# First head pair's bias loads on GpSimd's queue, and the fourth unit's exponentials ahead of the last value parts

## The chip, the cores and the metric

The program runs on one core of one Trainium2 chip. The metric is device microseconds (us) of one execution, as the median of several. TensorE (PE) multiplies matrices, VectorE (DVE), ScalarE (ACT) and GpSimd (POOL) work elementwise, SyncE (SP) here only issues DMAs. POOL and ACT can issue DMAs too. PEld is PE's loading of weights.

## The reference, cut to what matters

Attention with a bias that a small network computes from positions, then a feed-forward part with a convolution and a gate:

```python
scores = scale * np.matmul(q, k.transpose(0, 1, 3, 2))        # (4, 8, 576, 576)
x = (psi_rel / psi_i)[..., None]                              # (576, 576, 1)
h = np.maximum(x @ w1 + b1, 0.0)                              # 32 hidden units
scores = scores + (h @ w2).transpose(2, 0, 1)[None, :, :, :]  # a bias for each of 8 heads
attn = np.exp(scores - np.max(scores, axis=-1, keepdims=True))
attn = attn / (np.sum(attn, axis=-1, keepdims=True) + 1e-09)
x = np.matmul(attn, v)                                        # then heads are joined: (4, 576, 512)
h = np.maximum(x @ w_in, 0.0)
out = (h * sigmoid(conv3(h))) @ w_out
```

The bias does not depend on the batch. It is computed once, for all heads, and used four times.

## The kernel before, in words

**Bias stage.** A loop of 36 blocks (index i, `NBLK`) computes the bias, 16 rows of positions a block. For a block DVE (L250) and ACT (L246) compute four tiles `y` of hidden units, PE (L267) multiplies them by `w2` into PSUM, and for each pair of blocks ACT (L293) writes the result to a staging tile `st` (five of them in turn, one called `tl`), which SP stores to `bias_d` in HBM (L306, 607 KB a pair of blocks). The blocks are software-pipelined: in step i the program first emits the hidden tiles of block i+1, then the matmuls of block i, then `bias_out` of block i-1.

**Bias tiles.** Attention reads the bias back from HBM, as tiles `bt` of 128 rows for a head pair p and row group t = 0 to 4, by `load_bias(p, t)`: two DMAs, one for each head (L183 for t = 0, which has 64 rows for each head, 144 KB each; L181 for the others, 288 KB each). Row group 0 needs blocks 0 to 3, row group 1 blocks 4 to 11, and so on, so each load waits until the stores of its blocks have landed. For the first head pair the loads of t = 0 to 3 stand in the loop at i = 6, 14, 22 and 30 and are issued from SP; for the others POOL issues them. The load of (0, 4) comes after the loop, cut into rows 0 to 95 and 96 to 127.

**Units.** A unit (n, t) is a pair of heads of one batch (n) and a row group (t): PE's scores (L363), DVE's addition of the bias with the row maxima (`reduce`, L374, needs `bt`; it writes `sp` and `nm`), ACT's exponentials (`expo`, L388, one for each head), a small ACT copy that marks the tile as ready for PE (`turned_sp`, L342), PE's transposes (L422 into a PSUM tile shared with the scores of another unit, L434 into tiles `tp`), ACT's and DVE's copies of them to `ptx` and `pty` (L90, L93), and parts of the value product (L471). Four units of n = 0 are worked inside the bias loop, from steps 13, 21, 29 and 34: (0,0), (0,1), (0,2) and (0,3). Of (0,3), the fourth, the loop does only the scores and the two `reduce`.

**After the loop.** The program emits the scores and `reduce` of (1,0), then the value parts still in the deque `fill` (PE, L471, into a PSUM tile named `tp`; the last part ends with ACT's copy of it to `x`, L90 called from L480), then the exponentials of (0,3), then the main loop over `flat` = (0,3), (1,0), (1,1), (0,4), (1,2), ... In its turn u, that loop emits the scores and `reduce` of the unit two ahead, the transposes of unit u and the exponentials of the unit one ahead. Each engine works its instructions in the order in which they are emitted; nothing reorders them.

Of the kernel before, what the change touches and what calls it, by code (L numbers as in the profile page):

```python
# [19 lines left out]
def attention_ffn_kernel(  # L20
# [11 lines left out]
    nc = tc.nc  # L32
# [23 lines left out]
    def halves(ap):  # L56
        return ap.rearrange("p (a b) -> p a b", a=2)
# [79 lines left out]
    with tc.manual_schedule():  # L137
# [9 lines left out]
        def load(n):  # L147
            p, b = seq[n]
            qks[n] = t = q_p.tile([P, KO + S], F32, name="qk")
            keys = qk[b, p, :, KO:].rearrange("d (h a s) -> d a h s", h=2, a=2)  # L150
            for a in range(2):
                rows = slice(D * a, D * a + D)
                nc.sync.dma_start(t[rows, 0:KO], qk[b, p, :, 0:KO])
                nc.sync.dma_start(halves(t[rows, KO:]), keys[:, a])
# [10 lines left out]
        def load_v(n):  # L165
            p, b = seq[n]
            vts[n] = vt = v_t[n % 2]
            by5 = [x.rearrange("p (g s) d -> p g (s d)", s=5)[:, :, 0:4 * D] for x in (vt, v[b, p, :, 0:10])]
            nc.sync.dma_start(*by5)
            nc.sync.dma_start(vt[0:TL, 4], v[b, p, 0:TL, 4])  # L170
            nc.sync.dma_start(vt[TL:P, 9], v[b, p, TL:P, 4])

        def load_bias(p, t, cuts=()):
            queue = nc.gpsimd if p else nc.sync
            bt = bias_p.tile([P, 2, S], F32, name="bt") if t else bias0_p.tile([P, 1, S], F32, name="bt0")
            for a, e in zip((0,) + cuts, cuts + (P,)):
                for h in range(2):
                    c = (2 * p + h) * BW
                    if t:
                        i0 = TL + (t - 1) * P  # L180
                        queue.dma_start(bt[a:e, h], bias_rows[i0 + a:i0 + e, c:c + S])  # L181
                    else:
                        queue.dma_start(bt[TL * h:TL * h + TL, 0, :], bias_rows[0:TL, c:c + S])  # L183
            biast[p, t] = bt
# [52 lines left out]
        def bias_hidden(blk):  # L237
            full = max(reach(blk)[0], reach(blk)[1] + 1)
            ys = []
            for j in range(4):  # L240
                ig = 4 * blk + j
                n = max(S - 4 * ig, 4 * ig + 4) if 4 <= blk < 32 else full
                row = ybuf[blk % 4][:, j] if j < 3 else y3[:, blk % 4]
                y = row[:, 0:n]
                if j >= relu_from(blk):
                    nc.scalar.activation(  # L246
                        y, dist[:, 0:n], AF.Relu, bias=pars[:, 1:2], scale=inv[:, ig:ig + 1]
                    )
                else:
                    nc.vector.tensor_scalar(  # L250
                        y, dist[:, 0:n], inv[:, ig:ig + 1], nb1, op0=ALU.mult, op1=ALU.max
                    )
                ys.append(row[:, 0:full])
            return ys
# [3 lines left out]
        def bias_mm(blk, ys):  # L258
            n = ys[0].shape[1]
            if n > 512 or blk % 2 == 0:  # L260
                bias_ps[blk] = psS.tile([P, 2, 512], F32, name="s")
            else:
                bias_ps[blk] = bias_ps[blk - 1]
            ps = bias_ps[blk]
            for a in range(0, n, 512):
                for j in range(4):
                    nc.tensor.matmul(  # L267
                        ps[32 * j:32 * j + 32, a // 512 if n > 512 else blk % 2, 0:min(n - a, 512)],
                        w2b,
                        ys[j][:, a:min(n, a + 512)],  # L270
                        start=True,
                        stop=True,
                    )
# [55 lines left out]
        def new_sp(n, t):  # L329
            tag = f"sp{len(nms) % SPB}"  # L330
            tile = sp_p.tile([P, 2 * S + 2], F32, name="sp", tag=tag)
            if t:
                spt[n, t] = (tile[:, 0:2 * S].rearrange("p (h j) -> p h j", h=2), tag)
            else:
                if n == 0:
                    nc.vector.memset(tile[:, 0:TL], 0.0)
                    nc.vector.memset(tile[:, TL + S:P + S], 0.0)
                spt[n, t] = (tile[:, TL:TL + S].rearrange("p (h j) -> p h j", h=1), tag)

        def turned_sp(n, t):  # L340
            tile = sp_p.tile([P, 2 * S + 2], F32R, name="sr", tag=spt[n, t][1])
            nc.scalar.activation(tile[:, 2 * S:], pars[:, 0:2], AF.Copy)  # L342
            spt[n, t] = (tile, None)


        def scores(n, t, h):
            p, b = seq[n]
            qt = qks[n]
            if h == 0:
                if n not in sms:  # L350
                    sms[n] = sm_p.tile([P, 9], F32, name="sm")
                nms[n, t] = sm_p.tile([P, 2], F32, name="nm")
                new_sp(n, t)
            ps = psum["s"].tile([P, 2, 512], F32, name="s")


            ops = [(h, h * QW + P * t, slice(0, P))] if t else [
                (hh, hh * (QW + TL), slice(TL * hh, TL * hh + TL)) for hh in range(2)
            ]
            for hh, qo, po in ops:  # L360
                for a in range(2):
                    rows = slice(D * a, D * a + D)
                    nc.tensor.matmul(  # L363
                        ps[po, a, 0:HS],
                        qt[rows, qo:qo + po.stop - po.start],
                        qt[rows, KO + hh * HS:KO + hh * HS + HS],
                        start=True,
                        stop=True,
                    )
            return ps  # L370

        def reduce(ps, n, t, h):
            bt = biast[seq[n][0], t]
            nc.vector.tensor_tensor_reduce(  # L374
                out=halves(spt[n, t][0][:, h]),
                in0=ps[:, :, 0:HS],
                in1=halves(bt[:, h]),
                op0=ALU.add,
                op1=ALU.min,
                scale=-scale,  # L380
                scalar=3.0e38,
                accum_out=nms[n, t][:, h:h + 1],
            )

        def expo(n, t, h):
            sp, nm = spt[n, t][0], nms[n, t]
            col = 4 * h + t - 1 if t else 8
            exps[n, t, h] = nc.scalar.activation(  # L388
                sp[:, h], sp[:, h], AF.Exp, bias=nm[:, h:h + 1], scale=-1.0,
                accum_out=sms[n][:, col:col + 1],  # L390
            )
# [188 lines left out]
        flat = [(n, t) for n in range(1, NSEQ) for t in units]  # L580
# [4 lines left out]
        def heads(t):  # L585
            return (0, 1) if t else (0,)
# [26 lines left out]
        for i in range(NBLK):  # L613
            nxt = bias_hidden(i + 1) if i + 1 < NBLK else None
            bias_mm(i, hidden)
            if last:
                bias_out(*last)
            last = (i,)
            hidden = nxt
            if i % 8 == 6 % 8 and i >= 6:  # L620
                load_bias(0, (i - 6) // 8)
            if i == 2:
                load(0)
            if i == 4:
                load_v(0)
            if i == 16:
                load(1)
            if i == 20:
                load_v(1)
            if i in starts:  # L630
                unit = unit_steps(*first[starts.index(i)])
            if unit:
                next(unit, None)
            for _ in range(max(0, i - starts[-1] + 1)):
                fill.popleft()()
        bias_out(*last)
        load_bias(0, 4, (96,))
        reduce(scores(*flat[1], 0), *flat[1], 0)
        while fill:
            fill.popleft()()  # L640
        early.close()
        psT = pool(ctx, "psT", 3, space=PSUM)
        psO = pool(ctx, "psO", 1, space=PSUM)
        psum.update(s=psS, tp=psT, o=psO)
        for h in heads(flat[0][1]):
            expo(*flat[0], h)
        turned_sp(*flat[0])
        pv_share = (2, 2, 1, 3, 2)
        hs_ff = {}
        raw_w = {}  # L650
# [4 lines left out]
        for u, (n, t) in enumerate(flat):  # L655
            p, b = seq[n]
# [49 lines left out]
            if u + 2 < NU:  # L706
                n2, t2 = flat[u + 2]
                p2, b2 = seq[n2]
                if b2 == B - 1 and p2 + 1 < NP:
                    load_bias(p2 + 1, t2)  # L710
# [228 lines left out]
```

## Time and profile before

| | |
|---|---|
| median of 3 runs | 493.66 us (493.31 to 494.21) |
| profiled execution, its own time | 493.83 us |
| its span, first to last instruction | 492.1 us |
| granted TensorE clock, mean | 1.000 of full speed |
| PE / PEld / DVE / ACT / POOL busy | 478.5 / 353.1 / 376.9 / 311.4 / 154.0 us |
| DMA: SP's and POOL's queues | 47.02 MB and 12.77 MB, 33.2% and 8.8% of 16 DMA engines' span |

The busy times are sums over the whole span. The ends of matmuls are modelled, so that a busy PE is not one at its peak. Outside the span lie 1.7 us of the profiled execution.

### The profile page before, as it was taken

What the parts mean: (1) busy time and instruction counts of PE and PEld (TensorE: products, weight loads), DVE (VectorE), ACT (ScalarE), POOL (GpSimd) and SP (SyncE); (2) the same over time, 40 slices, a digit from 0 to 9 for tenths busy, and PEclk for the clock granted to TensorE, in tenths of its full rate; (3) what the DMA queues carried; (4) which work ended last, traced back from release to release, by engine and by line L of the source; (5) the groups of instructions that cost most, each with busy time, mean ns of one, the idle gap of its engine ahead of it and who ended that gap; (6) DMA issues with size and microseconds to landing.
All of it is one profiled execution on the core that took longest, in us unless ns stands there. A gap on an engine that the chain in (4) does not pass through costs nothing.

```text
span 492.1 us, 11067 instructions
## 1 busy us (share of the span) xinstructions
PE 478.5 (97%) x4202; PEld 353.1 (72%) x4202; DVE 376.9 (77%) x871; ACT 311.4 (63%) x751; POOL 154.0 (31%) x215
## 2 busy tenths in 40 slices
PE   6989999999999999999999999999999999999996
PEld 4333356666666666666666689889988999899986
DVE  6989967788898889988898729944896279838930
ACT  6989877888888889888888736712542144224510
POOL 1000001245455735565547725160081005400000
PEclk9999999999999999999999999999999999999999
DMA  1999667388667895589751300002000300020011
GB/s 38 280 332 318 253 194 172 93 277 214 158 180 201 225 254 157 161 218 290 191 130 50 111 25 26 2 0 87 0 1 0 108 1 1 1 85 1 1 44 64
DMA packets 32584, 60.82 MB, mean 124 GB/s; under 512 B 7196, under 2 KB 15796, under 8 KB 32532
## 3 DMA queue, kind: packets, MB, share of 16 engines
q1 hardware_dynamic: 27380, 47.02, 33.2%
q0 software_dynamic: 4768, 12.77, 8.8%
q8 instruction: 33, 0.54, 0.5%
q10 hardware_dynamic: 384, 0.35, 0.2%
q14 instruction: 19, 0.16, 0.1%
HBM read 44.12 MB, written 15.98 MB: 122 GB/s over the span
## 4 chain that ended last, share of the span: by engine, by line
PE 88%; ACT 5%; DVE 3%; DMA 3%; issue 1%; SPq 0%; DVEq 0%
PE s L536 21%; PE o L471 17%; PE s L363 16%; PE tp L786 16%; PE tp L434 9%; PE o L786 4%; PE s L267 2%; DVE y L250 2%; DMA bias_d<-st 1%; ACT st L293 1%; ACT y L246 1%; ACT sp L388 1%; PE s L422 1%; DVE sp L374 1%; DMA pars<-in_par_dram 1%; DMA bt<-bias_d 1%
## 5 line engine op out<-in xcount | busy, mean ns | idle before, releaser
L374 DVE CUSTOM_DVE_ANT_0 sp<-s,bt 128x576 f32<-128x576 f32 x144 | 104.1, 754 | 32.3 <-PE s L363 13.1
L388 ACT ACTIVATE sp<-sp,nm 128x576 f32<-128x576 f32 x144 | 109.9, 767 | 0.8 <-DVE nm L374 0.8
L536 PEld LDWEIGHTS s<-xs,wi 128*128 128x128 f32 x768 | 102.8, 189 | 1.2 <-issue 0.5
L536 PE MATMUL s<-xs,wi 128*128 128x288 f32 x768 | 103.6, 296 | 0.0
L363 PE MATMUL s<-qk 64*128 64x288 f32 (+1 forms) x640 | 92.6, 431 | 0.5 <-DVE pty L93 0.2
L363 PEld LDWEIGHTS s<-qk 64*128 64x128 f32 (+1 forms) x640 | 46.9, 175 | 42.1 <-DVE nm L374 12.1
L786 PE MATMUL tp<-wo,g 128*128 128x512 f32 x288 | 70.7, 390 | 0.0
L434 PE MATMUL tp<-identr,sr 64*128 64x64 f32 x1184 | 64.3, 247 | 0.0
L786 PEld LDWEIGHTS tp<-wo,g 128*128 128x128 f32 x288 | 53.7, 188 | 11.8 <-DVE g L781 0.9
L434 PEld LDWEIGHTS tp<-identr,sr 64*128 64x128 f32 x1184 | 55.5, 136 | 5.6 <-issue 0.6
L761 DVE SCALAR_TENSOR_TENSOR cv<-h,cw,cv 128x575 f32<-128x575 f32 x64 | 55.2, 863 | 2.5 <-ACT cv L756 0.6
L548 ACT ACTIVATE h<-s 128x576 f32<-128x576 f32 x32 | 20.8, 651 | 55.2 <-PE s L536 55.2
L267 PE MATMUL s<-y,pars 128*32 128x512 f32 (+8 forms) x352 | 46.8, 513 | 4.0 <-DVE y L250 3.4
L250 DVE TENSOR_SCALAR y<-tl,inv,nb 128x576 f32<-128x576 f32 (+33 forms) x112 | 47.6, 506 | 0.1
L471 PE MATMUL o<-ptx,vt 128*64 128x320 f32 x300 | 47.0, 442 | 0.0
L471 PE MATMUL o<-pty,vt 128*64 128x256 f32 x320 | 44.2, 393 | 0.0
L133 POOL TENSOR_SCALAR xs<-x 128x576 fp32r<-128x576 f32 x16 | 15.2, 950 | 81.4 <-PE s L536 66.5
L267 PEld LDWEIGHTS s<-y,pars 128*32 128x32 f32 x352 | 17.3, 115 | 30.6 <-DVE y L250 15.3
L767 ACT ACTIVATE cv<-cv 128x576 f32<-128x576 f32 x32 | 21.8, 680 | 23.6 <-DVE cv L761 23.6
L498 POOL DMA_DIRECT2D r_d<-rt x16 | 10.0, 625 | 82.9 <-DVE rt L93 82.9
L768 DVE SCALAR_TENSOR_TENSOR cv<-cv,h 128x576 f32<-128x576 f32 x32 | 29.6, 924 | 5.7 <-ACT cv L767 5.7
L93 DVE COPY ptx<-tp 128x256 f32<-128x256 f32 (+1 forms) x64 | 32.0, 499 | 1.4 <-PE tp L434 1.2
(83 smaller groups left out, 635.8 us busy)
## 6 DMA issues: line engine op xcount, KB each, us to landing
qk<-in_qk_dram SPq DMA_DIRECT2D x32, 320.0 KB, 5.1
bias_d<-st SPq DMA_DIRECT2D x13, 607.0 KB, 5.0
bt<-bias_d POOLq DMA_DIRECT2D x24, 288.0 KB, 5.5
qk<-in_qk_dram SPq DMA_DIRECT2D x32, 144.0 KB, 5.4
rb<-r_d POOLq DMA_DIRECT2D x32, 144.0 KB, 3.1
vt<-in_v_dram SPq DMA_DIRECT2D x16, 256.0 KB, 5.9
raw_w<-in_moe_w_in_dram SPq DMA_DIRECT2D x16, 256.0 KB, 5.0
out_dram<-o SPq DMA_DIRECT2D x16, 256.0 KB, 2.0
```

The lines of the kernel that those rows point to most:

```text
L93: nc.vector.tensor_copy(o, i)
L250: nc.vector.tensor_scalar(y, dist[:, 0:n], inv[:, ig:ig + 1], nb1, op0=ALU.mult, op1=ALU.max)
L267: nc.tensor.matmul(ps[32 * j:32 * j + 32, a // 512 if n > 512 else blk % 2, 0:min(n - a, 512)], w2b, ys[j][:, a:min(n, a + 512)], start=Tr ...
L363: nc.tensor.matmul(ps[po, a, 0:HS], qt[rows, qo:qo + po.stop - po.start], qt[rows, KO + hh * HS:KO + hh * HS + HS], start=True, stop=True,)
L374: nc.vector.tensor_tensor_reduce(out=halves(spt[n, t][0][:, h]), in0=ps[:, :, 0:HS], in1=halves(bt[:, h]), op0=ALU.add, op1=ALU.min, scale ...
L388: exps[n, t, h] = nc.scalar.activation(sp[:, h], sp[:, h], AF.Exp, bias=nm[:, h:h + 1], scale=-1.0, accum_out=sms[n][:, col:col + 1],)
L434: tr = nc.tensor.transpose(ps[a][:, TL * s:TL * s + TL].bitcast(F32R), spf[ra, j:j + P], identr[ra, ra])
L471: nc.tensor.matmul(po[D * h:D * h + D, 0:width], vt[:, slot, :], pt[:, blk, :], start=(c == 0), stop=(c == 4),)
L536: nc.tensor.matmul(ps[:, a, 0:HS], wi[c][:, pw, cs], xss[b, c][:, px, a * HS:(a + 1) * HS], start=(i == 0), stop=(i == 3 * KC - 1),)
L761: nc.vector.scalar_tensor_tensor(out=cv[:, o:o + S - 1], in0=h[:, i:i + S - 1], scalar=cw[:, f, kk:kk + 1], in1=cv[:, o:o + S - 1], op0=AL ...
L768: nc.vector.scalar_tensor_tensor(out=cv, in0=cv, scalar=1.0, in1=h, op0=ALU.add, op1=ALU.mult)
L786: nc.tensor.matmul(ps, lhs(f, gi), wo[f][:, wj, cs], start=(f == 0 and i == 0), stop=(f == FC - 1 and i == 2),)
```

## The change

Two edits. The queue of a bias load is now chosen by whether it is cut, so the four loads of the first head pair inside the loop go from SP's queue to POOL's, and they are emitted at i = 4, 12, 20, 28, two steps earlier. The cut load (0, 4) stays on SP. And the two exponentials of (0,3) with their `turned_sp` are emitted ahead of the value parts, no longer behind them.

```diff
         def load_bias(p, t, cuts=()):
-            queue = nc.gpsimd if p else nc.sync
+            queue = nc.sync if cuts else nc.gpsimd
...
-            if i % 8 == 6 % 8 and i >= 6:
-                load_bias(0, (i - 6) // 8)
+            if i % 8 == 4:
+                load_bias(0, i // 8)
...
         load_bias(0, 4, (96,))
         reduce(scores(*flat[1], 0), *flat[1], 0)
+        for h in heads(flat[0][1]):
+            expo(*flat[0], h)
+        turned_sp(*flat[0])
         while fill:
             fill.popleft()()
         early.close()
         psT = pool(ctx, "psT", 3, space=PSUM)
         psO = pool(ctx, "psO", 1, space=PSUM)
         psum.update(s=psS, tp=psT, o=psO)
-        for h in heads(flat[0][1]):
-            expo(*flat[0], h)
-        turned_sp(*flat[0])
```

SP's instructions in the first half of the bias loop, before (-) and now (+); `vt` is V, `st` and `tl` are staging tiles, L306 the stores, L183 and L181 the bias loads:

```order
 L171 DMA vt_106<-in_v_dram 64x64
 L306 DMA bias_d<-st_125 128x2x607
-L183 DMA bt_266<-bias_d 64x576 x2
 L306 DMA bias_d<-st_132 128x2x607 x2
 L306 DMA bias_d<-tl 128x2x607
 L306 DMA bias_d<-st_124 128x2x607
-L181 DMA bt<-bias_d 128x576 x2
 L306 DMA bias_d<-st_125 128x2x607
```

The stores keep their order, and the loads that stood between them are gone from SP.

POOL's instructions of the change at the same place, with what each waits for (DMAHW7 counts among others the store of blocks 2 and 3, DMAHW2 that of blocks 0 and 1); `rr` and `kv` are small constants, `r_d` belongs to the main loop:

```order
L318 MEMSET rr_155 128x128
L222 MEMSET kv 128x2
L183 DMA bt_243<-bias_d 64x576 [waits DMAHW7_49,DMAHW2_49]
L183 DMA bt_243<-bias_d 64x576
L181 DMA bt<-bias_d 128x576 [waits DMAHW5_49,DMAHW6_49,DMAHW4_49,DMAHW3_49]
L181 DMA bt<-bias_d 128x576
L181 DMA bt<-bias_d 128x576 [waits DMAHW6_49,DMAHW7_49,DMAHW5_49,DMAHW0_49]
L181 DMA bt<-bias_d 128x576
L181 DMA bt<-bias_d 128x576 [waits DMAHW4_49,DMAHW5_49,DMAHW3_49,DMAHW2_49]
L181 DMA bt<-bias_d 128x576
L498 DMA r_d<-rt 2x4x128 [waits DMASW0_49,DVE_49]
```

Between its constants and its first work of the main loop POOL had nothing; now it has these eight DMAs.

ACT's instructions at the end of the bias loop, before (-) and now (+); `x_121<-tp` is the copy behind the last value part, the second L388 with L342 is unit (1,0):

```order
 L293 ACTIVATE st_125<-s,kv 128x576
 L293 ACTIVATE st_125<-s,kv 128x31
+L388 ACTIVATE sp,sm<-sp,nm 128x576 x2
+L342 ACTIVATE sr<-pars 128x2
 L90 ACTIVATE x_121<-tp 128x320
-L388 ACTIVATE sp,sm<-sp,nm 128x576 x2
-L342 ACTIVATE sr<-pars 128x2
 L388 ACTIVATE sp,sm<-sp,nm 128x576
 L342 ACTIVATE sr<-pars 128x2
```

The three instructions of (0,3) pass the copy of `x`. PE's and DVE's orders are the same in both kernels.

## Rows read from the trace of the kernel before

**Rows 1.** Windows: length, busy time (instructions) by engine, clock, DMA share, GB/s.

```profile
12.00:27.00 15.00, 12.96 (x111) 4.61 (x103) 14.01 (x38) 14.20 (x25) 0.00 (x0) 1.00 0.94 296
...
66.00:76.00 10.00, 8.62 (x100) 5.88 (x100) 8.39 (x26) 9.83 (x29) 0.00 (x0) 1.00 0.52 130
76.00:100.00 24.00, 23.95 (x280) 15.94 (x280) 17.32 (x49) 17.91 (x49) 6.03 (x10) 1.00 0.57 138
```

**Rows 2.** Chain that ended last, 10 to 31 us: start, length, what.

```profile
14.64 7.12 DMA bias_d<-st
...
22.32 3.31 DMA bt<-bias_d
...
27.00 1.86 PE s L267 x8
```

**Rows 3.** Timeline of DVE, 19 to 27 us: start, length, instruction [idle before, releaser].

```profile
19.60 5.06 DVE L250 TENSOR_SCALAR y<-tl,inv,nb 128x400 f32<-128x400 f32 x13
...
25.80 0.76 DVE L374 CUSTOM_DVE_ANT_0 sp<-s,bt 128x576 f32<-128x576 f32 x1 [0.99 <-PE s L267]
```

**Rows 4.** Timeline of ACT, 18 to 27 us.

```profile
18.06 1.45 ACT L293 ACTIVATE st<-s,kv 128x960 f32<-128x960 f32 x2
```

**Rows 5.** Timeline of SP, 18 to 26 us.

```profile
23.00 1.05 SPq L306 DMA_DIRECT2D bias_d<-st  x2
```

**Rows 6.** Source line L183: minimum, median, maximum length in ns, first and last start.

```profile
L183 POOL DMA_DIRECT2D bt<-bias_d x6: 522/538/573, 96.1 to 212.8; - x6
```

**Rows 7.** The page, DMA issues: KB each, median us from issue to landing.

```profile
rb<-r_d POOLq DMA_DIRECT2D x32, 144.0 KB, 3.1
...
bt<-bias_d POOLq DMA_DIRECT2D x6, 144.0 KB, 4.8
```

**Rows 8.** DMA view, 22 to 28 us in 40 slices: busy share in tenths.

```profile
DMA  5321103608899297989999999999998999999999
```

**Rows 9.** Timeline of DVE, 100 to 180 us.

```profile
167.94 0.27 DVE L99 TENSOR_SCALAR wu<-raw_w 128x256 int32<-128x256 int32 x1
```

**Rows 10.** Timeline of POOL, 100 to 180 us.

```profile
167.78 1.13 POOL L181 DMA_DIRECT2D bt<-bias_d  x2
```

**Rows 11.** Timeline of all engines, 14 to 40 us: tile (0,1), its load and first use.

```profile
30.19 0.81 SPq L181 DMA_DIRECT2D bt<-bias_d  x2
...
37.12 0.76 DVE L374 CUSTOM_DVE_ANT_0 sp<-s,bt 128x576 f32<-128x576 f32 x1 [0.44 <-PE s L363]
```

**Rows 12.** Timeline of all engines, 56 to 80 us.

```profile
63.57 0.08 DVE L374 DVE_READ_ACCUMULATOR2_ANT nm<- 128x1 f32 x1
63.75 2.45 SPq L181 DMA_DIRECT2D bt<-bias_d  x4
...
65.86 1.24 PE L363 MATMUL s<-qk 64*128 64x288 f32 x8
66.01 0.44 ACT L90 ACTIVATE x<-tp 128x320 f32<-128x320 f32 x1 [2.88 <-PE tp L471]
...
66.77 0.76 DVE L374 CUSTOM_DVE_ANT_0 sp<-s,bt 128x576 f32<-128x576 f32 x1 [1.23 <-ACT x L90]
...
67.99 0.20 ACT L342 ACTIVATE sr<-pars 128x2 fp32r<-128x2 f32 x1
...
68.01 0.25 PE L422 MATMUL s<-identr,sr 64*128 64x64 f32 x2 [0.90 <-ACT sp L388]
...
68.30 0.76 DVE L374 CUSTOM_DVE_ANT_0 sp<-s,bt 128x576 f32<-128x576 f32 x1 [0.77 <-PE s L422]
...
69.78 0.75 DVE L374 CUSTOM_DVE_ANT_0 sp<-s,bt 128x576 f32<-128x576 f32 x1
```

**Rows 13.** DMA issues, 65.6 to 66.3 us: KB each, median us to landing.

```profile
bt<-bias_d SPq DMA_DIRECT2D x2, 72.0 KB, 3.2
```

**Rows 14.** Chain that ended last, 60 to 80 us.

```profile
76.05 0.72 PE s L363 x3
```

**Rows 15.** DMA issues, 160 to 180 us: KB each, median us to landing.

```profile
bt<-bias_d POOLq DMA_DIRECT2D x6, 288.0 KB, 8.4
```

## The prediction

> **What bounds the kernel now.** I read the busy times by stage first. From 12 to 27 us DVE and ACT are busy for 14.0 and 14.2 of 15 us and PE follows them; from 66 to 76 ACT is the fullest with 9.83 of 10; from 76 on it is PE, with 23.95 of 24 us [rows 1]. So time won or lost before 76 us reaches the end only if it moves the point where PE takes over, and then it stays, since PE has no idle time to absorb it.
>
> Second, the chain that ended last. Between 10 and 31 us it is not the engines alone. It runs through the store of blocks 2 and 3, which lands at 14.64 + 7.12 = 21.76, and through the load of the first bias tile, whose second half is on its way from 22.32 and lands 3.31 later, at 25.63; then the chain goes on over DVE to PE's matmuls at 27.00 [rows 2]. The reader should see the same in DVE's own rows. Its run of hidden tiles ends at 19.60 + 5.06 = 24.66, and the first `reduce` starts at 25.80 after 0.99 us of idling. That the row names PE as the releaser is no contradiction: the wait is for several things, and the chain shows the load as the last of them [rows 2, 3]. DVE is held up nowhere else by a bias load, so this load is the only one of the four moved ones that stands on the path.
>
> Third, the turn from the bias loop to the main loop. ACT idles 2.88 us up to 66.01, where it copies `x` behind the last value part. Only then come the two exponentials of (0,3), although the maxima that they need were read at 63.57 + 0.08 = 63.65. They are marked ready at 67.99 + 0.20, so PE idles 0.90 us before L422 at 68.01, and DVE, whose second `reduce` of (1,1) shares its PSUM tile with L422, idles 0.77 us up to 68.30 [rows 12]. From there DVE has no gap until the chain passes to PE at 76.05 [rows 14].
>
> **Part one: the four loads change queues.** What is removed is SP's waiting. In the loads' place SP stood waiting for the landing at 21.76 [rows 2], and the store of blocks 6 and 7, which ACT had ready at 18.06 + 1.45 = 19.51, left at 23.00 [rows 4, 5]. It can now go 3.5 us sooner. That pays nothing directly: no instruction of ACT, DVE or PE before 76 us is seen waiting for a store, a key or a value, only for this bias tile.
>
> "Two steps sooner" does not help the first tile either. Its DMA waited for the landing at 21.76, not for its turn in the program, and the store in question stands ahead of the change in SP's order, so it lands at 21.76 in both.
>
> What is added is POOL's way of issuing. One such DMA occupies POOL for 0.54 us [rows 6], so the second leaves at about 21.80 + 0.54 = 22.35, against 22.32 on SP. From there to landing the rows bound it on both sides. The shortest POOL transfers of this size, `rb`, take 3.1 us; the bias tiles of this very size on POOL take 4.8 [rows 7]. So it lands between 25.45 and 27.15, against 25.63: from 0.2 us sooner to 1.5 later. I take 4.5, near the upper row, because that row is the same transfer and because the lower one has quiet surroundings, which this place loses. The DMA view shows little moving between about 22.2 and 23.3, and the load has the DMA engines to itself there [rows 8]. That quiet came from SP standing still. With SP free, the store of blocks 6 and 7 and the next one fill it. Landing at 26.85 means that DVE starts 1.2 us later, and DVE, ACT and PE all wait behind that `reduce`: **+1.2 us**, bounds -0.2 and +1.5.
>
> The Trainium skill speaks against the edit here: "SBUF — State Buffer", section "SBUF: two separate sides", says that descriptors of a DMA issued from POOL are written by GpSimd, and that it cannot write them while DVE runs an operation in its two-port mode, since both share one port pair. By it this load would be late by far more than 1.2 us; what that would give is the first rival. The trace does not confirm it for a single operation: POOL's pair of DMAs at 167.78 takes 1.13 us, two times 0.54 and the usual gap, although DVE's tensor_scalar from SBUF to SBUF starts inside it at 167.94 and takes its usual 0.27 [rows 9, 10].
>
> The other three loads have room. Take (0,1): on SP its pair left from 30.19 on, so that with the 3.3 us of the first tile's half it had landed near 34, and it is needed at 37.12, where DVE waited only for PE [rows 2, 11]. Its stores now leave sooner. I cost the three at nothing; the cover is some 3 us, and what exceeds it would delay DVE one for one.
>
> **Part two: the exponentials of (0,3) go ahead.** ACT does the same work, which took from 66.45 to 68.19, so 1.74 us, but inside its 2.88 us of idling. It can start at 66.01 - 2.88 = 63.13 on the first head, the second head's maximum is there at 63.65, and so it is done by about 64.9, before the copy of `x` at 66.01, which keeps its time. So L422 no longer waits for ACT: it follows the scores, which end at 65.86 + 1.24 = 67.10, and starts about 0.9 us earlier. DVE's second `reduce` can start when L422 ends, at about 67.35, and when the first has ended, at 66.77 + 0.76 = 67.53, against 68.30: about 0.8 us sooner, and all of DVE's gapless run to 76 with it [rows 12].
>
> What is late next? The `reduce` of (0,4), at 69.78, would move to 69.0. Its tile comes by SP's four DMAs of 63.75 to 66.20; the last leaves at about 65.8 and lands 3.2 later, at 69.0 too, the half of the first head a little before [rows 12, 13]. So the tile just does not hold it back. Nor does ACT, which had been the fullest engine there and has 1.74 us less to do after 66. **-0.8 us**, bounds -0.9 (PE's whole gap) and -0.4 (the tile of (0,4) 0.4 later than that).
>
> **The sum.** The profiled execution took 493.83 us: 493.83 + 1.2 - 0.8 = 494.23. It lay 0.17 above the median of 493.66, so the forecast for a median is **494.1 us**. About 0.2% (1.0 us) is what a measurement of this kernel can tell from no change, and 0.4 is below it.
>
> **The rivals.** *POOL is shut out while DVE runs (slower).* The mechanism: thirteen hidden tiles run back to back to 24.66 [rows 3], POOL gets its turn only after them, and its second DMA lands at 24.7 + 0.54 + 4.8 = 30.0, 4.4 us late. With part two that is 493.66 + 4.4 - 0.8 = 497.3, more if it meets the load of (0,1) too. It decides from a delay of 1.8 us on (1.0 + 0.8). For it speaks the length of the run, against it the pair of rows above, though there was one operation and here are thirteen. 8%.
>
> *The transfer itself is slow (slower).* In a crowded stretch POOL's bias tiles needed 8.4 us [rows 15]. Here that lands at 30.75: 493.66 + 5.1 - 0.8 = 498.0. These were tiles of twice the size amid many small packets; but SP's freed stores do crowd the place. 7%.
>
> *The first tile comes no later (faster).* If POOL's transfer takes 3.1 us or less, part one pays 0.2 to at most 0.99 (DVE's whole idle time), and with part two the time is 492.7, at best 491.9. For it: the issue itself is not slower on POOL. Against: all bias tiles of this size there took near 4.8. 14%.
>
> *Part two is eaten up.* Should the tile of (0,4) come late because the last stores shift, 0.4 remains: 493.66 + 1.2 - 0.4 = 494.5. 9%.
>
> **How the numbers follow.** The forecast's own case holds 62%, from 493.5 (landing at 26.25, 0.6 late) to 494.8 (27.15 and part two at 0.4). Faster by over 0.2%: nearly all of the third rival, 0.13. Slower: the first two, half of the fourth, and 4% from the upper end of my own case, 0.24. The rest, 0.63, is no difference. A range that leaves out 2 in 10 goes below to 492.4, into the third rival, whose weight lies at its nearer end (some 5% stay out), and above to 496.2, short of the first two (15%).
>
> **What would show it.** In the profile after: POOL's L183 at about 21.8, the first `reduce` of DVE at 26.6 to 27.2 (25.80 before) with some 2 us of idling ahead of it; SP's store of blocks 6 and 7 near 19.5; ACT's two exponentials done before its copy of `x`; PE without the 0.90 us before L422; the step from DVE to PE about 0.4 us later than 76.05. It is wrong if the first `reduce` starts at or before 25.80, if it starts past 28, if a later load of the four holds DVE up, or if DVE idles ahead of the `reduce` of (0,4).

## The result and the profile after

| | before | changed kernel |
|---|---|---|
| median of five | 493.31 us (492.94 to 494.21) | 497.70 us (497.24 to 498.31) |
| span of the profiled execution | 492.1 us | 496.5 us |
| granted TensorE clock, mean | 1.000 | 0.995 |

The changed kernel is slower: ratio 1.0087, 95% interval 1.0075 to 1.0099, 4.4 us. The forecast was 494.1 us with a range up to 496.2; what came is the first rival, which had 8% and a price of 497.3. The number alone does not say so, for the second rival's 498.0 is as near to 497.70; the traces and the experiments below do. The profiled execution took 498.31 us, the longest of the five.

DVE's timeline of the changed kernel, 18 to 80 us, shows where the time goes. Columns as in [rows 3]: start, length, instruction, idle time before it and its releaser.

```profile
17.67 7.09 DVE L250 TENSOR_SCALAR y<-tl,inv,nb 128x428 f32<-128x428 f32 x18
24.71 0.11 DVE L336 MEMSET sp<- 128x64 f32 x1
...
29.57 0.76 DVE L374 CUSTOM_DVE_ANT_0 sp<-s,bt 128x576 f32<-128x576 f32 x1 [4.67 <-DMA bt<-bias_d]
...
34.05 0.67 DVE L93 COPY ptx<-tp 128x256 f32<-128x256 f32 x2 [1.20 <-PE tp L434]
...
41.73 0.76 DVE L374 CUSTOM_DVE_ANT_0 sp<-s,bt 128x576 f32<-128x576 f32 x1 [0.45 <-PE s L363]
...
71.37 0.76 DVE L374 CUSTOM_DVE_ANT_0 sp<-s,bt 128x576 f32<-128x576 f32 x1 [1.22 <-ACT x L90]
...
72.06 0.75 DVE L374 CUSTOM_DVE_ANT_0 sp<-s,bt 128x576 f32<-128x576 f32 x1
...
74.24 0.76 DVE L374 CUSTOM_DVE_ANT_0 sp<-s,bt 128x576 f32<-128x576 f32 x1 [0.62 <-PE tp L434]
```

Subtract the starts in [rows 3, 11, 12] from these. The first `reduce` comes 29.57 - 25.80 = 3.77 us late and has idled 4.67 us for its bias tile. At the `reduce` of (0,1) the delay is 41.73 - 37.12 = 4.61, so another 0.84 is lost between 30 and 41 us, but not at a load: that `reduce` waits for PE, as before. The delay is 4.60 at 71.37. At the next `reduce` it is 72.06 - 68.30 = 3.76: there part two wins its 0.84. At 74.24 it is 4.46 again. Four steps, then, and each has its row below.

Step one. POOL's timeline, 0 to 90 us (`x2` is the pair of one load):

```profile
22.07 3.32 POOL L183 DMA_DIRECT2D bt<-bias_d  x2 [19.65 <-DMA vt<-in_v_dram]
29.40 1.09 POOL L181 DMA_DIRECT2D bt<-bias_d  x2 [4.00 <-DMA bias_d<-tl]
48.72 1.22 POOL L181 DMA_DIRECT2D bt<-bias_d  x2 [18.23 <-DMA vt<-in_v_dram]
57.38 1.06 POOL L181 DMA_DIRECT2D bt<-bias_d  x2 [7.44 <-DMA bias_d<-st]
```

Source line L183: minimum, median and maximum length in ns, and the times from issue to landing.

```profile
L183 POOL DMA_DIRECT2D bt<-bias_d x8: 526/541/2789, 22.1 to 217.2; - x8
...
DMA to landing us min/median/max: 4.5/5.1/5.3
```

SP's timeline, 10 to 27 us, with the store of blocks 2 and 3, and DMA issues, 14.65 to 14.70 us, with its time to landing:

```profile
14.66 0.59 SPq L306 DMA_DIRECT2D bias_d<-st  x1
...
19.14 3.28 SPq L306 DMA_DIRECT2D bias_d<-st  x3
```

```profile
bias_d<-st SPq DMA_DIRECT2D x1, 607.0 KB, 6.8
```

The store that the load needs lands at about 14.66 + 6.8 = 21.5, a little sooner than the 21.76 of before. POOL begins some 0.6 us after that landing, where the forecast allowed 0.04 (21.80 against 21.76). (A load of V, which its row names, is only a DMA that counts on the same semaphore as a store.) So the pair starts near where it was forecast (22.07 for 21.80), but it takes 3.32 us in place of some 1.1. Seven of its kind on this line take about 0.54 and one takes 2.789: the first, which lasts to 22.07 + 2.79 = 24.86. DVE's run of hidden tiles ends at 17.67 + 7.09 = 24.76. So the second DMA leaves at 24.86 in place of 22.35, and with the shortest landing of the line, 4.5 us, the tile is there at 29.4, just ahead of the `reduce`.

Step two. A window of the changed kernel (columns as in [rows 1]):

```profile
30.00:34.00 4.00, 3.24 (x22) 1.50 (x26) 2.85 (x9) 1.50 (x4) 0.49 (x1) 0.58 0.49 157
```

And PE's timeline, 22 to 35 us:

```profile
30.76 2.46 PE L267 MATMUL s<-y,pars 128*32 128x352 f32 x8 [5.17 <-DVE y L250]
33.16 0.83 PE L434 MATMUL tp<-identr,sr 64*128 64x64 f32 x10
```

While DVE waits, PE runs dry and stands 5.17 us. After it the granted clock is 0.58 of full speed over 30 to 34 us, a mixture of the two levels, 1.2 and 2.4 GHz. The eight matmuls of L267 take 2.46 us, against 1.86 in [rows 2], and DVE waits for what follows them. That is the growth of the delay from 3.77 to 4.61, and DVE's row at 34.05 shows it as a wait of 1.20 for PE. In the kernel before that wait was 0.35, and PE stood 1.48 us, with a granted clock whose mean over the whole execution is 1.000 (DVE's timeline, 25 to 30 us; PE's, 22 to 42):

```profile
29.43 0.67 DVE L93 COPY ptx<-tp 128x256 f32<-128x256 f32 x2 [0.35 <-PE tp L434]
```

```profile
27.00 1.86 PE L267 MATMUL s<-y,pars 128*32 128x352 f32 x8 [1.48 <-DVE y L250]
```

Step three, part two. All engines, 66 to 82 us; ACT's two lines are the mark of (0,3) behind its exponentials and the copy of `x`:

```profile
69.28 0.20 ACT L342 ACTIVATE sr<-pars 128x2 fp32r<-128x2 f32 x1
...
70.47 1.24 PE L363 MATMUL s<-qk 64*128 64x288 f32 x8
70.59 0.44 ACT L90 ACTIVATE x<-tp 128x320 f32<-128x320 f32 x1 [1.11 <-PE tp L471]
...
71.33 0.41 PE L422 MATMUL s<-identr,sr 64*128 64x64 f32 x2
```

The tile of (0,3) is marked at 69.48, a microsecond before `x` is copied. PE's 0.90 us ahead of L422 and DVE's 0.77 ahead of the second `reduce` of [rows 12] are gone.

Step four. The starts of the four DMAs of tile (0,4) on SP (source line L181); DMA issues, 70.4 to 70.7 us (KB each, us to landing), which shows the last of the four; the chain that ended last, 60 to 90 us (its first piece on PE); and PE's row of `p2_only`, part two alone, from its timeline of all engines, 62.5 to 70.2 us:

```profile
L181 SPq DMA_DIRECT2D bt<-bias_d x4: 302/378/434, 68.3 to 70.3; - x4
```

```profile
bt<-bias_d SPq DMA_DIRECT2D x1, 72.0 KB, 3.9
```

```profile
80.51 0.72 PE s L363 x3
```

```profile
68.25 0.72 PE L434 MATMUL tp<-identr,sr 64*128 64x64 f32 x9
```

The load of (0,4) is cut by rows, so its last two DMAs, of 72 KB each, bring rows 96 to 127 of the two heads. The last of them took 3.9 us to land, against 3.2 for these DMAs in [rows 13], and the `reduce` that needs the tile idles 0.62 at 74.24. The row names PE's L434 as the releaser, but in `p2_only` the same `reduce` starts at 68.33 (its row stands below), 0.08 us after these matmuls have begun, so it does not wait for their end. The last DMA of the load left at 70.3 and landed 3.9 later, at 74.2, so the wait is for the load. In this one execution, which took 0.6 more than the median of the five, 0.70 of part two's 0.84 is lost again there. The chain passes to PE at 80.51, 4.46 after the 76.05 of [rows 14], and from there PE has no room: the span is 4.4 longer.

### The profile page after: what moved, and what is told of

Its sections match the earlier page's. It is cut to its first block, busy times and chain, and to the rows that moved or that the text cites. A ratio compares the mean times of both kernels' runs of the same rounds, so it can differ in the third digit from the quotient of the medians.

```text
span 496.5 us, 11065 instructions
## 1 busy us (share of the span) xinstructions
PE 479.2 (97%) x4202; PEld 353.1 (71%) x4202; DVE 377.8 (76%) x871; ACT 311.8 (63%) x751; POOL 160.1 (32%) x223
## 4 chain that ended last, share of the span: by engine, by line
PE 83%; DVE 1%; issue 0%; DVEq 0%
PE s L536 21%; PE o L471 17%; PE tp L786 16%; PE s L363 15%; PE tp L434 9%; PE o L786 4%; PE s L422 1%; DVE sp L374 1%; DVE ptx L93 0%; PE s L426 0%; DVE o L794 0%; PE tp L491 0%; DVE rr L487 0%; DVE pty L93 0%; PE tp L565 0%
## 5 line engine op out<-in xcount | busy, mean ns | idle before, releaser
L374 DVE CUSTOM_DVE_ANT_0 sp<-s,bt 128x576 f32<-128x576 f32 x144 | 104.0, 754 | 35.5 <-PE s L363 13.2
L388 ACT ACTIVATE sp<-sp,nm 128x576 f32<-128x576 f32 x144 | 109.9, 767 | 4.6 <-DVE nm L374 4.6
L786 PE MATMUL tp<-wo,g 128*128 128x512 f32 x288 | 70.7, 390 | 0.0
L434 PE MATMUL tp<-identr,sr 64*128 64x64 f32 x1184 | 64.6, 248 | 0.0
L434 PEld LDWEIGHTS tp<-identr,sr 64*128 64x128 f32 x1184 | 55.8, 136 | 6.3 <-issue 1.1
L267 PE MATMUL s<-y,pars 128*32 128x512 f32 (+8 forms) x352 | 47.4, 514 | 7.7 <-DVE y L250 7.1
L250 DVE TENSOR_SCALAR y<-tl,inv,nb 128x576 f32<-128x576 f32 (+33 forms) x112 | 47.6, 500 | 0.1
L267 PEld LDWEIGHTS s<-y,pars 128*32 128x32 f32 x352 | 17.0, 115 | 34.7 <-DVE y L250 19.3
L767 ACT ACTIVATE cv<-cv 128x576 f32<-128x576 f32 x32 | 21.8, 680 | 23.6 <-DVE cv L761 23.6
L93 DVE COPY ptx<-tp 128x256 f32<-128x256 f32 (+1 forms) x64 | 32.0, 499 | 2.2 <-PE tp L434 2.0
L90 ACT ACTIVATE ptx<-tp 128x256 f32<-128x256 f32 (+1 forms) x64 | 26.4, 437 | 7.9 <-PE tp L434 7.3
```

Of the source, the lines that this page charges most:

```text
L93: nc.vector.tensor_copy(o, i)
L250: nc.vector.tensor_scalar(y, dist[:, 0:n], inv[:, ig:ig + 1], nb1, op0=ALU.mult, op1=ALU.max)
L267: nc.tensor.matmul(ps[32 * j:32 * j + 32, a // 512 if n > 512 else blk % 2, 0:min(n - a, 512)], w2b, ys[j][:, a:min(n, a + 512)], start=Tr ...
L374: nc.vector.tensor_tensor_reduce(out=halves(spt[n, t][0][:, h]), in0=ps[:, :, 0:HS], in1=halves(bt[:, h]), op0=ALU.add, op1=ALU.min, scale ...
L388: exps[n, t, h] = nc.scalar.activation(sp[:, h], sp[:, h], AF.Exp, bias=nm[:, h:h + 1], scale=-1.0, accum_out=sms[n][:, col:col + 1],)
L434: tr = nc.tensor.transpose(ps[a][:, TL * s:TL * s + TL].bitcast(F32R), spf[ra, j:j + P], identr[ra, ra])
```

## Experiments

Times stand beside executions of the kernel before on the same chip, 493.09 to 493.38 us. The theories: **shut out** (a run of hidden tiles on DVE keeps POOL from issuing until it ends; then the stall of PE lowers its clock), against **slow transfer** (POOL's transfer is slow or crowded, the second rival) and, for part two, **eaten up** (the tile of (0,4) takes the gain back).

### The two parts apart

`p1_only` is the queue edit alone, on the kernel before:

```diff
-            queue = nc.gpsimd if p else nc.sync
+            queue = nc.sync if cuts else nc.gpsimd
...
-            if i % 8 == 6 % 8 and i >= 6:
-                load_bias(0, (i - 6) // 8)
+            if i % 8 == 4:
+                load_bias(0, i // 8)
```

> The queue edit alone, the exponentials left where they were. Theory S (POOL cannot issue its DMA while DVE runs hidden tiles back to back) and theory C (the freed stores crowd the DMA engines) both leave the first tile late: 493.3 + 4.4 plus what part two is worth, so 497.9 if part two brings 0.2 us and 498.5 if it brings the 0.8 forecast; first reduce at 29.6.

Measured: 498.52 us (498.12 to 498.56), ratio 1.0099 [1.0085, 1.0112], 5.1 us slower. POOL's timeline:

```profile
22.23 3.23 POOL L183 DMA_DIRECT2D bt<-bias_d  x2 [19.81 <-DMA vt<-in_v_dram]
```

`p2_only` is the other edit alone, on the kernel before:

```diff
         reduce(scores(*flat[1], 0), *flat[1], 0)
+        for h in heads(flat[0][1]):
+            expo(*flat[0], h)
+        turned_sp(*flat[0])
         while fill:
...
         psum.update(s=psS, tp=psT, o=psO)
-        for h in heads(flat[0][1]):
-            expo(*flat[0], h)
-        turned_sp(*flat[0])
```

> The exponentials alone, all loads of the first head pair back on SP. Forecast of part two: 493.3 - 0.8 = 492.5. Rival (the tile of (0,4), whose last DMA took 4.0 us to land in the changed kernel, holds DVE up): 493.1, with DVE idling ahead of the reduce of (0,4).

Measured: 492.50 us, ratio 0.9978 [0.9970, 0.9986], 0.9 us faster. DVE's timeline, 18 to 72 us:

```profile
66.76 0.75 DVE L374 CUSTOM_DVE_ANT_0 sp<-s,bt 128x576 f32<-128x576 f32 x1
...
68.33 0.76 DVE L374 CUSTOM_DVE_ANT_0 sp<-s,bt 128x576 f32<-128x576 f32 x1
```

The loss lies in the queue edit by itself. Part two gives what it was forecast to give alone, and the `reduce` of (0,4) at 68.33 follows without idling. In the changed kernel the medians give the same (498.52 - 497.70 = 0.8), though the intervals of these two ratios overlap.

### Which of the four loads

`first_on_sp` is the changed kernel with only the first tile's load back on SP, at its old place:

```diff
-            queue = nc.sync if cuts else nc.gpsimd
+            queue = nc.gpsimd if t and not cuts or p else nc.sync
...
-            if i % 8 == 4:
+            if i % 8 == 4 and i > 4:
                 load_bias(0, i // 8)
+            if i == 6:
+                load_bias(0, 0)
```

> The changed kernel with only the load of row group 0 put back on SP at i = 6; row groups 1 to 3 stay on POOL at i = 12, 20, 28. If only the first tile does the harm: the time of part two alone, 492.5 to 493.1, first reduce at 25.8. If POOL's queue harms the later tiles too: over 494, with DVE idling ahead of a reduce of (0,1), (0,2) or (0,3).

Measured: 492.97 us, ratio 0.9988 [0.9980, 0.9997]. DVE's timeline, 17 to 72 us, shows the first `reduce` without idling for its tile, and no later `reduce` idling for one:

```profile
24.95 0.76 DVE L374 CUSTOM_DVE_ANT_0 sp<-s,bt 128x576 f32<-128x576 f32 x1
```

The loss is in the first tile's load. The other three hold nothing up in this trace, as forecast. The median lies 0.5 above that of `p2_only`, with intervals that overlap; whether the three cost part of that stays open.

### Does the issue last as long as DVE's run

`start16` is the changed kernel with the first unit begun three steps later, so that DVE's run goes on for three more blocks before the first `reduce` interrupts it:

```diff
-        starts = [13, 21, 29, 34]
+        starts = [16, 21, 29, 34]
```

> The changed kernel with the first unit started at step 16 in place of 13, so that three more blocks of hidden tiles come ahead of its reduce. Theory S, strict: POOL stays shut out to the end of the longer run, its first DMA lasts about 6 us, DVE idles some 4.7 us as before, time 497.6. Theory C, or an S that is let through by gaps: the tile lands at about 27 to 30, near the end of the run, DVE idles 1 us or less, time 492.8 to 493.8.

Measured: 497.59 us, ratio 1.0083 [1.0070, 1.0096]. POOL's timeline, and DVE's from 17 us on:

```profile
22.26 6.65 POOL L183 DMA_DIRECT2D bt<-bias_d  x2 [19.84 <-DMA vt<-in_v_dram]
```

```profile
16.81 11.46 DVE L250 TENSOR_SCALAR y<-tl,inv,nb 128x440 f32<-128x440 f32 x30
...
33.28 0.76 DVE L374 CUSTOM_DVE_ANT_0 sp<-s,bt 128x576 f32<-128x576 f32 x1 [4.86 <-DMA bt<-bias_d]
```

POOL starts at 22.26, 0.2 later than in the changed kernel. But the first issue now takes 6.12 us by its source line, to 28.38, and DVE's run ends at 28.27. The issue stretches with the run. A slow transfer would have left the issue at 0.54.

`oneport` keeps the changed kernel and computes DVE's hidden tiles of blocks 12 to 14 by another instruction with two tensor inputs (the same values; lines below move by six, L250 to L251 or L256, L374 to L380):

```diff
-                    nc.vector.tensor_scalar(
-                        y, dist[:, 0:n], inv[:, ig:ig + 1], nb1, op0=ALU.mult, op1=ALU.max
-                    )
+                    if blk in (12, 13, 14):
+                        nc.vector.scalar_tensor_tensor(
+                            out=y, in0=dist[:, 0:n], scalar=inv[:, ig:ig + 1],
+                            in1=nb1.to_broadcast([P, n]), op0=ALU.mult, op1=ALU.max
+                        )
...
```

> The changed kernel with DVE's nine hidden tiles of blocks 12 to 14 computed by scalar_tensor_tensor with a broadcast second input, the same values, in place of tensor_scalar. Each should be some 0.2 us longer. Theory S: POOL's first DMA of row group 0 takes 0.55 us, not 2.79, the tile lands at about 27, DVE idles less than 1.5 us, time 494 to 495.5. Theory C: the first reduce is at 29.5 or later and the time 497.7 or more.

Measured: 495.88 us, ratio 1.0057 [1.0043, 1.0072]. POOL's and DVE's timelines:

```profile
22.33 1.24 POOL L183 DMA_DIRECT2D bt<-bias_d  x2 [19.90 <-DMA bias_d<-st]
```

```profile
20.82 5.13 DVE L251 SCALAR_TENSOR_TENSOR y<-tl,inv,nb 128x384 f32<-128x384 f32 x10
...
27.90 0.76 DVE L380 CUSTOM_DVE_ANT_0 sp<-s,bt 128x576 f32<-128x576 f32 x1 [1.80 <-DMA bt<-bias_d]
```

DVE is just as busy and its run as unbroken, but POOL's pair, which lies in the middle of it, is back at 1.24 us. In the eight other traces in which POOL issues inside the run ahead of the first `reduce`, all with tensor_scalar, it is held until that run ends. So it is not DVE's work as such that shuts POOL out here, but the form of the hidden tiles' instruction. Nor is it that this is POOL's first DMA, which it is here too. The second DMA leaves at about 23.0, and the tile lands some 4.7 later, near the upper of the two landing times that the prediction had.

The time is a little above what was expected. DVE's run is 1.2 us longer with the other instruction, but that costs nothing here, since DVE idles 1.80 behind it. The cost is PE's clock once more. A window, PE's timeline, 22 to 36 us, and DVE's, 18 to 45 us:

```profile
30.00:34.00 4.00, 3.93 (x26) 1.30 (x24) 2.76 (x9) 1.86 (x7) 1.29 (x2) 0.58 0.46 149
```

```profile
29.09 2.46 PE L273 MATMUL s<-y,pars 128*32 128x352 f32 x8 [2.30 <-DVE y L256]
```

```profile
40.06 0.76 DVE L380 CUSTOM_DVE_ANT_0 sp<-s,bt 128x576 f32<-128x576 f32 x1 [0.44 <-PE s L369]
```

The first `reduce` is 27.90 - 25.80 = 2.10 late, the `reduce` of (0,1) 40.06 - 37.12 = 2.94. Here PE had stood only 2.30 us, and the step costs 0.84 all the same. With part two's 0.84 taken off, 2.1 us remain, and 493.83 + 2.1 = 495.9 agrees with the 495.88 measured.

`pool_extra` adds to the kernel before one POOL DMA that nothing uses; it can go as soon as blocks 0 and 1 are stored:

```diff
             if i == 2:
+                nc.gpsimd.dma_start(rr_t[1][0:32], bias_rows[0:32, 0:P])
                 load(0)
```

> The kernel before with one more DMA on POOL, unused by anything: 32 rows by 128 of the bias of blocks 0 and 1 into a scratch tile, which waits for their store to land, at about 15 us, inside DVE's long run from 13.7 to 24.7. Theory S: this one instruction lasts until DVE's run ends, about 9 us. If POOL is let through between DVE's instructions it lasts 0.5 to 1.5 us. Time 493.3 by both, unless POOL's writing slows DVE: then more.

Measured: 493.34 us, ratio 1.0006 [0.9996, 1.0016]. POOL's timeline, and DVE's:

```profile
14.88 9.99 POOL L623 DMA_DIRECT2D rr<-bias_d  x1 [12.46 <-DMA bias_d<-tl]
```

```profile
9.74 15.02 DVE L250 TENSOR_SCALAR y<-tl,inv,nb 128x544 f32<-128x544 f32 x36
```

One issue of 9.99 us, ended at 24.87, again 0.1 after the run's end at 24.76. And the wait is one-sided: DVE loses nothing by it, and the time is that of before.

### What PE's clock costs

`pe_warm` and `pe_warm5` add ten and five matmuls, which nothing uses, to the changed kernel at step 13, to keep PE from standing still (shown with five):

```diff
+            if i == 13:
+                junk = psB.tile([P, 512], F32, name="tp")
+                for _ in range(5):
+                    nc.tensor.matmul(junk[0:32, 0:512], w2b, dist[:, 0:512], start=True, stop=True)
```

> The changed kernel with ten unused matmuls on PE behind the scores of the first unit, which fill some 4 us of its wait. If the granted clock of 0.58 from 30 to 34 us comes of PE's standing still and costs the 0.85 us by which the delay grows from 3.77 to 4.62: clock 1.00 there, time 496.9. If the 0.85 has another source: 497.7.

Measured with ten: 499.25 us, ratio 1.0124 [1.0110, 1.0138]. The ten matmuls took over 8 us and ran past the landing of the tile, so PE itself was late. The clock stayed at 1.00, but nothing follows for its cost.

> The changed kernel with five unused matmuls on PE behind the first unit's scores (ten took 8.3 us and ran past the wait; five take 4.2, from 25.5 to 29.7, inside it). If the lower clock behind the wait is what makes 4.62 us out of 3.77: clock 1.00 from 30 to 34 us and 496.9. If not: 497.7.

Measured with five: 496.87 us, ratio 1.0076 [1.0061, 1.0092]. A window, and DVE's timeline:

```profile
30.00:34.00 4.00, 3.05 (x26) 1.18 (x26) 3.60 (x12) 2.44 (x8) 0.16 (x1) 1.00 0.46 151
```

```profile
29.47 0.76 DVE L374 CUSTOM_DVE_ANT_0 sp<-s,bt 128x576 f32<-128x576 f32 x1 [4.73 <-DMA bt<-bias_d]
...
33.10 0.67 DVE L93 COPY ptx<-tp 128x256 f32<-128x256 f32 x2 [0.35 <-PE tp L434]
```

The first `reduce` is as late as in the changed kernel, but the clock is 1.00 and the step from it to L93 is 33.10 - 29.47 = 3.63 us in place of 34.05 - 29.57 = 4.48. That is 0.85, and the step is then that of the kernel before (29.43 - 25.80 = 3.63). The time falls by 497.70 - 496.87 = 0.8; the intervals of these two ratios overlap, so that the rows carry this reading and the medians only agree with it.

### Is part two held back by the tile of (0,4)

`tile4_early` is part two alone, with the tile (0,4) loaded in the loop, at i = 33. So early its own rows are not there yet; it takes those of row group 3, and the kernel leaves out the right bias for row group 4:

```diff
-        def load_bias(p, t, cuts=()):
+        def load_bias(p, t, cuts=(), rows_of=None):
...
-                        i0 = TL + (t - 1) * P
+                        i0 = TL + ((rows_of or t) - 1) * P
...
+            if i == 33:
+                load_bias(0, 4, (96,), 3)
...
-        load_bias(0, 4, (96,))
```

> Part two alone, with the tile of (0,4) loaded at i = 33 from the rows of row group 3, so that it cannot be late; the bias of row group 4 of the first head pair is the wrong one. If that tile's landing eats part two: 492.5, 0.5 or more below part two alone, no idling ahead of the reduce of (0,4). If something else eats it: the time of part two alone.

Measured: 492.79 us, ratio 0.9984 [0.9975, 0.9994], nothing better than the 492.50 of `p2_only`. So in part two alone the landing of this tile is early enough, by as little as the prediction's working had it (69.0 against 69.0). That the changed kernel's profiled execution lost 0.62 us near it is the thin side of this margin.

### When does POOL get through

The later loads of `first_on_sp` start inside runs of hidden tiles too, and yet they pass. `pool_probe` adds sixteen small POOL DMAs that nothing uses to the kernel before, one for each pair of blocks:

```diff
+            if i % 2 == 0 and i >= 2 and i < NBLK - 2:
+                nc.gpsimd.dma_start(rr_t[1][0:32, 4 * i - 8:4 * i], bias_rows[16 * (i - 2):16 * (i - 2) + 32, 0:8])
```

> The kernel before with sixteen more small DMAs on POOL, each waiting for one pair of blocks to land, their data unused: a row of lengths over the whole bias stage. If every back-to-back run of hidden tiles shuts POOL out, one DMA in each run lasts to the run's end (2 to 6 us). If only the run before the first reduce does, whose instructions wait for PE or for nothing, the first lasts from about 15 to 24.9 and all later ones 0.5 to 1 us, as the loads of row groups 1 to 3 did with row group 0 back on SP (0.54 to 0.87 each).

Measured in one execution: 493.15 us, no different from before. POOL's timeline:

```profile
15.05 10.70 POOL L619 DMA_DIRECT2D rr<-bias_d  x3 [12.62 <-DMA bias_d<-tl]
...
29.90 0.69 POOL L619 DMA_DIRECT2D rr<-bias_d  x1 [1.28 <-DMA bias_d<-tl]
31.92 4.62 POOL L619 DMA_DIRECT2D rr<-bias_d  x2 [1.33 <-DMA bias_d<-st]
```

Two runs of DVE shut POOL out, not one: the first DMA takes 9.69 us, and the first of the pair from 31.92 on takes 4.08, to 36.00, the end of the run that goes from 29.36 to 35.90. Source line L619 between 31.5 and 35.9 us, and DVE's timeline:

```profile
L619 POOL DMA_DIRECT2D rr<-bias_d x1: 4081/4081/4081, 31.9 to 31.9; - x1
```

```profile
29.36 6.54 DVE L250 TENSOR_SCALAR y<-tl,inv,nb 128x304 f32<-128x304 f32 x18
```

The DMA at 29.90 lies in the same run and passes in 0.69, and others pass in two later runs. What set the runs apart in the order of the program was their waits: tiles that wait for PE where POOL was shut out, tiles that wait only for DVE's own earlier writes where it mostly passed. `own_wait` tries that: a tiny DVE copy in the changed kernel makes nine of the ten hidden tiles of blocks 12 to 14 wait for DVE itself.

```diff
+            if i == 11:
+                seen = bias_c.tile([P, 1], F32, name="seen")
+                nc.vector.tensor_copy(seen, bias_ps[10][:, 0, 0:1])
             nxt = bias_hidden(i + 1) if i + 1 < NBLK else None
```

> The changed kernel with one tiny DVE copy (128x1, out of a PSUM tile of block 10) ahead of the hidden tiles of block 12. It is the only work added. Since DVE has then seen PE's progress, the nine hidden tiles of blocks 12 to 14 no longer wait for PE but for DVE's own earlier writes; their number, widths and operation stay as they are. Theory that the wait decides (runs whose instructions wait for DVE itself let POOL through): the first L183 takes 0.5 to 0.9 us in place of 2.79 and the pair 1.1 to 1.7 in place of 3.32, the first reduce starts at 27.5 to 28.3, and the time is 495 to 496.2. Rival, that any back-to-back run of these tiles shuts POOL out: the first L183 again ends with DVE's run near 24.8 to 25.2, the first reduce starts at 29.5 to 29.9, and the time is 497.2 to 498.2. Should the copy itself be what lets POOL in, the issue ends at the copy, near 21, before it could start.

Measured: 497.65 us (495.59 to 499.16), ratio 1.0088 [1.0054, 1.0122]. POOL's and DVE's timelines:

```profile
21.67 3.61 POOL L183 DMA_DIRECT2D bt<-bias_d  x2 [19.25 <-DMA vt<-in_v_dram]
```

```profile
20.76 3.87 DVE L250 TENSOR_SCALAR y<-tl,inv,nb 128x384 f32<-128x384 f32 x10
```

The first issue takes 3.08 us by its source line, from 21.67 to 24.75; the run ends at 24.63. The theory of the waits falls: POOL is shut out all the same. Why some runs let it through stays open.

### A better version

Part two alone, with the first unit one step later, so that DVE's run covers the landing of its tile (all loads on SP):

```diff
-        starts = [13, 21, 29, 34]
+        starts = [14, 21, 29, 34]
```

> All loads of the first head pair on SP as before, the exponentials moved as in the change, and the first unit started at step 14 in place of 13. The first tile's landing at 25.1 to 25.6 then falls inside DVE's run, which ends one block (1.2 us) later: no idling ahead of the first reduce, 0.3 to 1.0 us below part two alone: 491.5 to 492.2. Rival: the units' later steps crowd and nothing is won: 492.5.

Measured: 492.26 us, ratio 0.9978 [0.9969, 0.9987]. DVE's timeline:

```profile
68.35 0.76 DVE L374 CUSTOM_DVE_ANT_0 sp<-s,bt 128x576 f32<-128x576 f32 x1 [0.50 <-DMA bt<-bias_d]
```

The first `reduce` no longer waits, but the `reduce` of (0,4) now idles 0.50 for its tile, and the ratio is that of `p2_only`: 492.26 lies between what was expected (491.5 to 492.2) and the rival (492.5). Either version is 0.2% faster than the kernel before.

## Why the prediction was wrong

**The step that failed** is in part one: "One such DMA occupies POOL for 0.54 us [rows 6], so the second leaves at about 21.80 + 0.54 = 22.35". The issue took 2.79 us. All bounds behind it were put on the way from issue to landing, and none on the issue, though the working named a rule that speaks of the issue. A second term, PE's clock behind the delay, was put at nothing without a word, and took 0.85. Of the term's 3.77 us, 2.25 are the longer issue (2.79 - 0.54), some 0.3 the later start (22.07 against about 21.8), and 1.2 the slower landing (4.5 against 3.31 in [rows 2]). The 1.2 is the +1.2 that was forecast; its size was right, and it was the smaller part. The reason given for it, crowding by SP's freed stores, is not shown: the transfers of L183 land 5.1 us after their issue in the median, and three of its four pairs come after the bias loop. Nor were the two landing times that bound it extremes, for each was the median of a group.

**Why the rival got 8%.** The sum set one pair of rows [rows 9, 10] against a run of thirteen instructions [rows 3]. `start16` and `oneport` show that here the length of the run and the form of its instruction decide; one operation of 0.27 us, on int32, inside a pair that is 1.13 long was no test, since a delay of that size or less hides in it. Other rows of the same DVE line, in the kernel before, show that the two engines do hold each other up. Source line L99, and the timeline of all engines, 139 to 141 us:

```profile
L99 DVE TENSOR_SCALAR wu<-raw_w x28: 271/294/1534, 106.0 to 259.7; 128x256 int32<-128x256 int32 x28
```

```profile
139.16 1.52 POOL L511 TENSOR_TENSOR x<-x,rb 128x576 f32<-128x576 f32 x1
...
139.29 1.53 DVE L99 TENSOR_SCALAR wu<-raw_w 128x256 int32<-128x256 int32 x1
```

The tile that takes 0.29 us in the median takes 1.53 beside an elementwise instruction of POOL's, until 0.14 after that one ends (140.82 against 140.68).

The Trainium skill gives a cause in "SBUF — State Buffer", section "SBUF: two separate sides": a DVE operation in its two-port mode has the shared port pair to itself until it ends, and a DMA issued from POOL cannot have its descriptors written meanwhile. The same section reports a blocked DMA to be released about 115 ns after DVE's end. The traces agree in the time: the first issue ends 0.10 to 0.12 us after the run in the changed kernel, `start16`, `pool_extra` and `own_wait`. That the port is what holds POOL, no run here shows by itself. And it is a whole run that holds it, not one instruction: in `pool_extra` POOL finds no opening in the last 9.9 us of a run in which 36 instructions take 15.02, so between some two dozen of them. Why it finds one at once in other runs (`pool_probe`) stays open.

**The price of the rival** was 497.3, and 497.7 was measured. Its landing was put at 30.0 and came at 29.4. What it lacked was PE's clock after the stall, 0.85, which `pe_warm5` gives back. The forecast's own case had this term at nothing too. In `oneport` the first `reduce` comes only 2.10 late, PE stands 2.30 us, and the clock costs as much; with the forecast's 1.2, PE's 1.48 us of idling in the kernel before grow to some 2.7 (an estimate, 1.48 + 1.2), so that the forecast's own case would probably have paid it too. No run shows that case itself.

**The other three loads** were costed at nothing, and in the trace of `first_on_sp` nothing waits for them. **SP's waiting** ended as forecast and paid nothing: three of its stores, that of blocks 6 and 7 among them, leave between 19.14 and 22.42, where that one had left at 23.00 [rows 5].

**Part two** was forecast at -0.8 and measured at -0.9 alone and -0.8 in the changed kernel. The fourth rival, the tile of (0,4), shows in single executions (0.62 us here, 0.50 in `best14`), and `tile4_early` shows that it takes nothing measurable from the median of part two alone. So two of the prediction's own signs of being wrong came: a first `reduce` past 28, and DVE idling ahead of the `reduce` of (0,4).

**The sum again**, with what was measured: 3.77 + 0.85 - 0.84 + 0.70 = 4.48 at PE's start, and 4.46 is read there. Only the 0.85 comes from another execution; the other terms are differences along the same two traces, so the agreement tells that no step is missing and no more. The medians of `p1_only` say 5.1 for part one, half a microsecond more than the 4.6 of these rows. The first `reduce` of the kernel before idled 0.99 us in its profiled execution, but 0.30 in that of `p2_only` and not at all in that of `first_on_sp`, with the same load on SP. So the execution from which the sum was made was late at this very place, and may have made part one look cheaper by up to that much.

## What to carry to other kernels

Before a load moves from SP's queue to POOL's, look at what DVE does at the moment when the load becomes ready: behind an unbroken run of SBUF-to-SBUF tensor_scalar tiles, POOL's issue may last until the run ends (up to 9.99 us here), so price it at the end of the run and not at the median issue. A load on which the first work after such a run depends stays on SP; loads with slack may move. And when a delay leaves PE idle for some microseconds, add the slower matmuls behind it to the price: 0.85 us here after 5.17 us, and as much in `oneport` after 2.30.

## What was not expected of the hardware

An issue that takes 0.54 us took 2.79, 6.12, 9.69 and 9.99 us, always to about 0.1 us after the end of DVE's run, while the kernel with the 9.99 was no slower (ratio 1.0006): there the one who waits is POOL alone. The same values computed by scalar_tensor_tensor let the pair through in 1.24 us.

Not every run of the same instruction shuts POOL out. `pool_probe` has one DMA that passes in 0.69 us at 29.90 and one that is held for 4.08 from 31.92 on, in the same run; the waits of DVE's instructions do not explain it (`own_wait`). This stays open.

After PE had stood 5.17 us, the granted clock over 30 to 34 us was 0.58, and eight matmuls took 2.46 us in place of 1.86. After 2.30 us in `oneport` it was 0.58 over the same stretch, and the eight took 2.46 again.
